# Four layers of linear and memory attention in one kernel: weight stores in pieces, one reciprocal later, the last block by quarters

## The chip, the cores and the metric

The kernel runs on one NeuronCore of a Trainium2 chip. The metric is the device time of one execution in microseconds (us), lower is better. The engines are named as in the profile: PE (TensorE, matrix products and transpositions), DVE (VectorE), ACT (ScalarE), POOL (GpSimd) and SP (SyncE, whose queue issues nearly all DMAs). PE, DVE, ACT and POOL each run their instructions in order.

## What is computed

`x` is 2048 tokens by 512 features in fp32. Four layers follow each other, A, B, A, B, with the same weights for both A and both B, and each adds its result to `x`:

```
x = x + A(layernorm(x));  x = x + B(layernorm(x));  x = x + A(layernorm(x));  x = x + B(layernorm(x))

A (32 heads of 16):  q, k, v = x @ wqkv;  pq, pk = q @ w_phi, k @ w_phi   (16 x 16 per head)
   phi = [softmax(p), softmax(-p)];  kv = phi_k^T v;  z = sum of phi_k
   o = (phi_q kv) / (phi_q z + 1e-6);  result o @ wo

B (32 heads of 16, 4 segments of 512 tokens):  q, k, v = x @ wq, x @ wk, x @ wv;  phi(t) = t + 1 or exp(t)
   in a segment:  a_dot = softmax(q k^T / 4, causal) v;   a_mem = (phi(q) M) / (phi(q) z + 1e-6)
   o = g a_mem + (1 - g) a_dot;   M += phi(k)^T v;  z += phi(k);   result o @ wo
```

## The kernel before

Products that must be exact to fp32 are done as three products of high and low parts (`mm3`, L465: high x high, high x low, low x high); the high part is a copy on ACT, the low part a subtraction on DVE or POOL. All work of the four layers is one stream for PE. Instructions of DVE, ACT, POOL and SP go through the helper `Ordered` (L161; every one of them bears the line L171 in the profile), and products through `mm` (L190, line L193) or `tp` (L195, line L197), which keep the order in which the program issues them. So the program's order is the engines' order, and it is written out by hand.

**Banks.** Of the eight PSUM banks, three bear the tag `g` (projections, transpositions, outputs), `lg` takes two (one tile of 128 x 1024 logits), and `mx`, `my` and `pv` one each.

**A layers.** `pass1` (L682) goes through the segments in the order 1, 2, 3, 0: values, keys, queries, features, and `kv` (L752) sums into `mx` and `my`. In the first A layer `first` (L618) splits the weights `awv`, `awk`, `awq` into high and low parts, and puts (store, tile) pairs of 1 MB into the list `owed` (L631); `settle` (L271) issues stores from it, one at every fourth step of the segment with n = 1 (L809). `prepare` (L320) meanwhile splits and stores the B layers' weights. In the second A layer these weights come back through `load_w` (L248), which goes through the whole of `bring` (L254) at once: eight loads of 256 KB. This second A layer starts under the end of the first B layer: `pass1` is then the generator `after`, from which the table `LAST` takes steps ("ln", "v", "n").

**B layers.** A segment s has four chunks c of eight heads and each chunk two halves: m = 0 to 31 counts (s, c, half). Five steps k belong to each m (R = 5, 160 in all). In every step `attend` (L1214) makes one block of logits into `lg`, ACT takes the exponential of 128 x 1024, and POOL masks the diagonal. Nine steps ahead `maxima` (L1172) makes the same logits per query in `mx` and `my` and takes maxima of them on DVE ("junk" and "mx" in the profile, result `mxs`), which `put_maxima` (L1205) turns and adds to the queries as a further row. `weighted` (L1250) multiplies the exponentials with the values into `pv`: key blocks 0 and 3 at step 5(m+1), blocks 1 and 2 two steps later (L1477); then ACT scales `pv` to `U`.

The denominators make a way through DRAM: `gather` (L1093) stores `U`'s rows, and `invert` (L1064) loads them compactly (`dm`, or `dn` when the memory's go along), inverts them on DVE (`flip`), stores the inverse (`put`), copies it wide (`spread`) and loads it wide (`load`). `INVERT` (L50) has the steps of these five, the first row for all segments but the last; half steps are those after the step's table entries (`due(k + 0.5)`, L1495). POOL then multiplies and joins (`close`, L1102, times in `JOIN`), and `out` (L1318) multiplies with the output weights.

In the last segment the chunks c >= 2 go another way: `finish` (L1283) turns `U` on PE, takes the reciprocal of the turned denominators on DVE and multiplies; `end_turn` (L1296) turns back, adds the memory's part, and splits into high and low; `early` (L1330) makes the last segment's output products over the first three chunks beforehand, and `end` (L1346) those over the last chunk, adds and stores. After the last step the end is: `finish` of m = 31, the rest of `early`, `end_turn(3)`, `end` (L1499 to 1511), with steps of the next layer between them.

**The tables** `FIRST`, `GAPS`, `LAST`, `FINAL` (L59 to 109) name for each step "m.j" the other work: "k2/3" is three of four parts of the key projection of chunk 2, "~" puts its subtraction behind, "max" is `put_maxima`, "n", "ln", "N" are steps of the normalisation, "t" and "a", "m" belong to the memory, "out", "p", "pt", "fin" to the outputs, "w" loads two pieces of the output weights, "v" in `LAST` is a step of `after`. `steps` (L1372) goes through them.

Of the kernel before, what the change touches and what calls it, by code (L numbers as in the profile page):

```python
# [17 lines left out]
DH = 16  # L18
# [41 lines left out]
0.1 max k2/2       | 0.2 v3/2          | 0.3 k2~  # L60
0.4 v3             | 1.0 m0            | 1.1 max q3/2      | 1.3 q3~           | 1.4 t1 k3/1
2.1 max k3         | 2.2 m1            | 2.3 ln~           | 2.4 ln~ ln~
3.3 q0+/2          | 3.0 w
3.1 max ln~        | 3.4 t2 q0+~ w
4.0 w | 5.2 w
4.1 max k0+/2 load | 4.2 m2            | 4.3 k0+/1         | 4.4 k0+
5.0 n              | 5.3 q1+/2 n
5.1 max v0+        | 5.4 t3 q1+~       | 6.2 m3 n
6.1 max v1+        | 6.3 k1+/2
6.4 a0+ k1+        | 7.0 n             | 7.2 n  # L70
7.1 max q2+~       | 7.3 v2+/2 n       | 7.4 t0+ v2+
"""
GAPS = """
0.1 max k2/3       | 0.2 n             | 0.3 k2~ v3/2 n
0.4 a1 v3          | 1.0 m0 n
1.1 max q3/3       | 1.2 n             | 1.3 q3~ k3/2      | 1.4 t1 k3~
2.1 max out/3      | 2.2 m1            | 2.3 ln ln         | 2.4 a2 ln x0
3.1 max ln out~    | 3.3 q0+/3 x1      | 3.4 t2 q0+~ k0+/2
4.1 max k0+~ out/1 load                | 4.2 m2            | 4.3 out~ x2
4.4 a3 q1+~  # L80
5.0 n              | 5.1 max out/3     | 5.3 out v0+/2 n x3
5.4 t3 v0+ k1+/1
6.1 max k1+~       | 6.2 m3 n          | 6.3 out/3
6.4 a0+ out v1+/2  | 7.0 n
7.1 max v1+ q2+/1 begin                | 7.2 n             | 7.3 q2+~ n N
7.4 t0+ v2+ N
# [3 lines left out]
0.1 max k2/3       | 0.2 n             | 0.3 k2~ v3/2 n  # L90
0.4 a1 v3 n        | 1.0 n             | 1.2 n
1.1 max q3/3 n     | 1.3 q3~ k3/2 n    | 1.4 k3~ n
2.1 max out/2      | 2.3 out/1         | 2.4 a2 x0
3.1 max ln~ ln~    | 3.3 out ln~ out/1 x1 | 3.4 out/1 ln~
4.1 max out~ v/2   | 4.3 out/3 x2      | 4.4 a3 out~ v x3
5.1 max out/3      | 5.3 fin out v/2   | 5.4 v pre
6.1 max v/2        | 6.3 fin v         | 6.4 v/2
7.1 pt p v         | 7.3 fin v/2 p     | 7.4 p v
"""
FINAL = """  # L100
0.1 max k2~        | 0.3 v3/3          | 0.4 a1 v3
1.1 max q3/2       | 1.3 q3~           | 1.4 k3/1
2.1 max k3/2       | 2.3 k3 out/1      | 2.4 a2 out/2 x0
3.1 max            | 3.3 out/2 x1      | 3.4 out/2
4.1 max out~       | 4.3 out/3 x2      | 4.4 a3 out/1
5.1 max out/2 x3   | 5.3 fin out~      | 5.4 pre
6.1 max            | 6.3 fin           | 6.4
7.1 pt p           | 7.3 fin p         | 7.4 p
"""
BEFORE = {-25: "q0 load", -23: "v0", -21: "k0",  # L110
          -18: "n", -17: "v1 n", -16: "n", -15: "n n", -14: "q1 n", -13: "n", -12: "k1 n", -11: "n", -10: "v2 n",
          -4: "max q2~", -1: "t0"}
# [3 lines left out]
def interleave_kernel(ctx, tc, x_in, a_wqkv, a_wphi, a_wo, b_wq, b_wk, b_wv, b_wo, b_beta,  # L116
# [496 lines left out]
    class LayerA:  # L613
# [4 lines left out]
        def first(self, hT, vv, upcoming):  # L618
# [63 lines left out]
        def pass1(self, first):  # L682
# [277 lines left out]
    class LayerB:  # L960
# [289 lines left out]
        def weighted(self, m, last):  # L1250
# [3 lines left out]
            if not last:  # L1254
                self.pv[m] = PS("pv", PV)
# [316 lines left out]
```

## Time and profile before

| | us |
|---|---|
| three runs | 1453.22, 1457.74, 1453.77; median 1453.77 |
| profiled execution | 1457.08, of it span 1455.4 |
| first A layer, to about | 260 |
| first B layer, about | 260 to 756 |
| second A layer, about | 756 to 1010 |
| second B layer, about | 1010 to 1455 |

All times in what follows count from the span's start. A row of the timeline has start, duration, engine, line, operation, output <- input by the program's names and the shape, and in square brackets the engine's idle time before it with what ended it. A row of the waits has the engine and what it wrote, what it waited for, and total, count and longest. A row of the windows has the stretch, its length, busy time (and instructions) of PE, PE's weight loads, DVE, ACT and POOL, then PE's granted clock as a share of full speed, the DMA engines' share and GB/s. "SPq" is a DMA issue on SP's queue. The profile calls weight tiles of the first A layer `w` or `e` by their buffers, the sum over keys `my<-P,v`.

### The profile page before, as it was taken

Reading aid. Unit: us, or ns where it says so; the run is one execution under the profiler, and the core shown is the slowest. Engines: PE = TensorE matmul, PEld = TensorE weight load, DVE = VectorE, ACT = ScalarE, POOL = GpSimd, SP = SyncE. Lnnn points to the kernel's source line nnn. Section 1 sums busy time; section 2 is a strip of 40 time slices with the busy share of each in tenths; the row PEclk is TensorE's granted clock in tenths of the full one; section 3 lists DMA queues with packets and bytes.
Section 4 is the critical chain, followed back from the end, with each engine's and each line's share of the span. In section 5 each row is a group of like instructions: output and inputs, shape, how many; then the busy total and the mean of one; then the engine's idle time right before and its main releaser. Section 6 shows DMA issues by size and latency. Waiting matters only on the chain.

```text
span 1455.4 us, 33122 instructions
## 1 busy us (share of the span) xinstructions
PE 1384.2 (95%) x12052; PEld 954.6 (66%) x12052; DVE 951.7 (65%) x3007; ACT 809.4 (56%) x1228; POOL 733.3 (50%) x1066
## 2 busy tenths in 40 slices
PE   7989999999999999998999998999999999999987
PEld 6878778765556565665568887886655566566544
DVE  4766788677467557566547767959756665666662
ACT  5546345447576576565544434553656865765653
POOL 1558765325456556444424456641445555654543
PEclk9999999999999999999999999999999999999999
DMA  5376475536546556566531103854465565556552
GB/s 191 117 290 233 138 234 171 177 115 191 165 139 211 170 150 201 153 181 201 184 136 55 59 30 112 274 185 134 120 197 149 150 213 172 156 173 185 143 167 72
DMA packets 139793, 236.34 MB, mean 162 GB/s; under 512 B 26576, under 2 KB 40016, under 8 KB 138864
## 3 DMA queue, kind: packets, MB, share of 16 engines
q1 hardware_dynamic: 138480, 233.70, 52.2%
q8 instruction: 97, 1.59, 0.4%
q10 hardware_dynamic: 1152, 0.52, 0.1%
q14 instruction: 64, 0.52, 0.1%
HBM read 129.17 MB, written 55.18 MB: 127 GB/s over the span
## 4 chain that ended last, share of the span: by engine, by line
PE 74%; DVE 7%; DMA 6%; ACT 6%; POOL 3%; issue 2%; SPq 1%; ACTq 0%; POOLq 0%; DVEq 0%
PE g L193 46%; PE pv L193 8%; PE lg L193 8%; PE mx L193 4%; PE g L197 4%; PE my L193 3%; ACT P L171 2%; PE lg L197 2%; SPq L171 1%; POOL P L171 1%; DVE junk L171 1%; DMA KN<-wide 1%; POOL tmp L171 1%; DMA dm<-den 1%; ACT tb L171 1%
## 5 line engine op out<-in xcount | busy, mean ns | idle before, releaser
L171 ACT ACTIVATE P<-lg 128x1024 f32<-128x1024 f32 x320 | 329.0, 1028 | 178.1 <-PE lg L193 164.3
L171 POOL TENSOR_SCALAR_AFFINE_SELECT P<-P 128x256 f32<-128x256 f32 (+1 forms) x448 | 191.2, 442 | 404.1 <-ACT P L171 403.3
L171 DVE CUSTOM_DVE_ANT_0 junk<-mx,mask 128x128 uint8<-128x128 f32 (+2 forms) x384 | 146.7, 420 | 124.2 <-PE my L193 93.4
L193 PE MATMUL g<-hh,wqk 128*128 128x512 f32 x512 | 186.3, 412 | 0.7 <-ACT mt L171 0.7
L193 PE MATMUL lg<-e,e 64*128 64x256 f32 (+2 forms) x1024 | 169.2, 388 | 14.4 <-ACT P L171 14.0
L193 PE MATMUL g<-w,oh 128*128 128x512 f32 x512 | 172.7, 419 | 4.4 <-ACT oh L171 4.0
L193 PE MATMUL pv<-P,v 128*32 128x512 f32 (+3 forms) x2048 | 167.2, 444 | 5.1 <-ACT ot L171 5.1
L171 DVE CUSTOM_DVE_ANT_0 mx<-mx,mask 128x512 f32<-128x512 f32 x128 | 89.1, 696 | 109.5 <-PE my L193 91.4
L193 PEld LDWEIGHTS lg<-e,e 64*128 64x128 f32 x1024 | 81.5, 185 | 114.4 <-issue 54.6
L193 PE MATMUL mx<-e,e 63*128 63x256 f32 (+2 forms) x512 | 145.5, 337 | 9.1 <-DVE mxs L171 8.5
L193 PE MATMUL my<-e,e 63*128 63x256 f32 (+2 forms) x512 | 147.3, 348 | 4.9 <-DVE mxs L171 3.7
L171 DVE CUSTOM_DVE_ANT_0 junk<-my,mask 128x128 uint8<-128x128 f32 (+2 forms) x384 | 146.8, 420 | 0.2 <-PE g L193 0.2
L193 PE MATMUL g<-w,hh 128*128 128x512 f32 x448 | 145.5, 406 | 0.0
L193 PEld LDWEIGHTS pv<-P,v 128*32 128x32 f32 x2048 | 55.0, 110 | 109.2 <-issue 95.8
L193 PEld LDWEIGHTS g<-hh,wqk 128*128 128x128 f32 x512 | 97.2, 190 | 31.8 <-issue 10.5
L193 PEld LDWEIGHTS g<-w,oh 128*128 128x128 f32 x512 | 90.0, 192 | 32.9 <-issue 11.0
L193 PE MATMUL g<-w,ol 128*128 128x512 f32 x256 | 103.8, 406 | 3.8 <-DVE ol L171 2.5
L193 PEld LDWEIGHTS mx<-e,e 63*128 63x128 f32 x512 | 90.0, 187 | 18.4 <-DVE mxs L171 7.3
L193 PE MATMUL g<-hl,wqk 128*128 128x512 f32 x256 | 101.1, 395 | 0.0
L171 DVE DVE_READ_ACCUMULATOR2_ANT mxs<- 128x1 f32 x1024 | 100.1, 98 | 0.0
L193 PEld LDWEIGHTS g<-w,hh 128*128 128x128 f32 x448 | 82.2, 192 | 22.6 <-issue 6.0
L193 PEld LDWEIGHTS my<-e,e 63*128 63x128 f32 x512 | 84.0, 187 | 17.9 <-DVE mxs L171 9.1
(167 smaller groups left out, 2820.9 us busy)
## 6 DMA issues: line engine op xcount, KB each, us to landing
e<-ta SPq DMA_DIRECT2D x384, 128.0 KB
wqk<-wqk SPq DMA_DIRECT2D x64, 512.0 KB
x<-x SPq DMA_DIRECT2D x48, 256.0 KB
wide<-inv SPq DMA_DIRECT2D x20, 512.0 KB
xr<-x SPq DMA_DIRECT2D x32, 256.0 KB
x<-xr SPq DMA_DIRECT2D x28, 256.0 KB
tmp<-U SPq DMA_DIRECT2D x56, 128.0 KB
KN<-wide SPq DMA_DIRECT2D x28, 256.0 KB
```

The costliest lines, as they stand in the source:

```text
L171: i = f(*a, **k)
L193: return held(nc.tensor.matmul(*a, **k))
L197: return held(nc.tensor.transpose(*a))
```

## The change

1. `owed` gets pieces of 256 KB (24 in place of 6 of 1 MB), and they are stored at every third step in the segments n = 1 and 2.
2. `INVERT` has three rows. For the first segment `flip` is at 4 and not 3.5: eight reciprocals of `dm`, four in each B layer, stand behind the four "junk" maxima that they stood ahead of. The steps of the other segments stay.
3. The second A layer's `awv` comes in pieces: from the 12th step of its normalisation on two loads of 256 KB a step, between SP's other DMAs.
4. `kv(0)` of an A layer's last segment is one projection earlier (`KV`).
5. Tables: the number of parts is written out everywhere; the first piece of the output weights comes at 2.2 and not at 3.0 of `FIRST`, one "n" of `GAPS` a few steps later, "max" ahead of or behind its neighbour in two cells.
6. `WEIGHTS`: of m = 30 the blocks 1, 2 come one step after 0, 3 (and not two); of m = 31 block 0 two steps, blocks 3 and 1 one step before the end of the steps, block 2 at it.
7. `final`, the second B layer alone: of the last eight blocks of logits every second goes to `mx` and `my`, with two exponentials of 128 x 512.
8. `close_last` takes the place of `finish(31)`, `end_turn(3)` and `end` in both B layers: `U`, the transpositions, reciprocals, sums and splits of the last chunk go in quarters of 128 tokens, in the order of `TAIL`.

DVE gets 24 instructions more, ACT 16, SP 18; PE and POOL have as many as before. The diff without the rewritten tables, where those change only as said in 5:

```diff
-INVERT = ((2.5, 3.5, 4.5, 5.5, 7.5), (2.5, 4.5, 5.5, 6.5, 8.5))
+INVERT = ((2.5, 4, 4.5, 5.5, 7.5), (2.5, 3.5, 4.5, 5.5, 7.5), (2.5, 4.5, 5.5, 6.5, 8.5))
+TAIL = "p o0 p o1 p o2 p t0 p o3 p t1 P a0 t2 a1 t3 a2 a3"
+WEIGHTS = {-2: ((0, (0, 3)), (1, (1, 2))), -1: ((-2, (0,)), (-1, (3, 1)), (0, (2,)))}
+SECOND = 9
+EARLY = (0, 1, 2)
+WV = 12
+SPREAD = 3
+KV = (4, 6)
...
-                owed.extend(zip(kept[key], w))
+                owed.extend((k[:, kc, :], t[:, kc, :]) for k, t in zip(kept[key], w) for kc in range(NC))
...
                 norm = norm_T(self.xsrc, SEGS[0], hTs, slow=True, off=True)
-                for _ in range(11):
-                    next(norm)
+                wv = []
+                weights = bring(wv, "awv")
+                for n, _ in enumerate(norm):
                     yield
-                wv = load_w("awv")
-                for _ in norm:
-                    yield
+                    if n + 1 >= WV:
+                        next(weights, None)
+                for _ in weights:
+                    pass
...
-                        if n == 1 and i % 4 == 0:
+                        if n in (1, 2) and i % SPREAD == 0:
                             settle(1)
...
-                    if t in (5, 6):
-                        add = kv(t - 5)
+                    if t in KV:
+                        add = kv(KV.index(t))
...
-                self.invert(s, c, k + READ[2], range(1, 2), INVERT[1])
+                self.invert(s, c, k + READ[2], range(1, 2), INVERT[2])
...
-            self.invert(s, c, k, range(2 if s > 0 else 1), INVERT[s == NSEG - 1])
+            self.invert(s, c, k, range(2 if s > 0 else 1), INVERT[0 if s == 0 else 2 if s == NSEG - 1 else 1])
...
-            for kbs, r in (((0,), 0), ((0,), 1), ((1, 3), 0), ((1, 3), 1), ((2,), None)):
-                pb = PS("lg", 1, (P, 2, 512))
+            for n, (kbs, r) in enumerate((((0,), 0), ((0,), 1), ((1, 3), 0), ((1, 3), 1), ((2,), None))):
+                left = R * 8 * NSEG - R * m - n
+                if self.final and left < SECOND and left % 2 == 0:
+                    pb = [PS(tag, 1) for tag in ("mx", "my")]
+                else:
+                    pb = PS("lg", 1, (P, 2, 512))
...
-                    act.activation(pr, pb, AF.Exp, scale=0.25)
+                    for part in enumerate(pb) if isinstance(pb, list) else ((slice(0, 2), pb),):
+                        act.activation(pr[:, part[0]], part[1], AF.Exp, scale=0.25)
...
-                U = T2("U", 2)
-                act.activation(U, self.pv.pop(m), AF.Identity, scale=share[:, m % 8 : m % 8 + 1])
+                U, pv = T2("U", 2), self.pv.pop(m)
+                for part in range(4 if m == 8 * NSEG - 1 else 1):
+                    cut = slice(part * P, part * P + P) if m == 8 * NSEG - 1 else slice(0, 512)
+                    act.activation(U[:, cut], pv[:, cut], AF.Identity, scale=share[:, m % 8 : m % 8 + 1])
...
+        def close_last(self, rest):
+            s, c, hf = NSEG - 1, NC - 1, 1
+            U, ot, old = self.U.pop(8 * NSEG - 1), self.ot.pop(c), self.old.pop((s, c))
+            hi, lo = self.oT[s, c] = self.outputs(s, c)
+            banks = [PS("mx", 1), PS("my", 1)]
+            wide = PS("lg", 1, (P, 2, 512))
+
+            def own(t):
+                cut = slice(t * P, t * P + P)
+                pt = banks[t % 2][:, t // 2 * P : t // 2 * P + P]
+                tp(pt, U[:, cut], ident)
+                r = T2("r", 4, shape=(P, 4, 4))[:, 0]
+                dve.reciprocal(r, pt.rearrange("p (h e) -> p h e", h=4)[:, :, 31 * hf])
+                dve.tensor_tensor(out=ot.rearrange("p q (h d) -> p q h d", d=DH)[:, t, 4 * hf : 4 * hf + 4], op=MUL,
+                                  in0=pt.rearrange("p (h d x) -> p h d x", h=4, x=2)[:, :, :, 1 - hf],
+                                  in1=r.unsqueeze(2).broadcast_to([P, 4, DH]))
+
+            def turned(t):
+                cut = slice(t * P, t * P + P)
+                pt = wide[:, t % 2, t // 2 * P : t // 2 * P + P]
+                tp(pt, ot[:, t], ident)
+                dve.tensor_tensor(out=old[:, cut], in0=pt, in1=old[:, cut], op=ADD)
+                act.copy(hi[:, cut], old[:, cut])
+                dve.tensor_tensor(out=lo[:, cut], in0=old[:, cut], in1=hi[:, cut].bitcast(F32), op=SUB)
+
+            def added(t):
+                po = PS("g", G)
+                for _ in self.product(po, s, t, range(NC - 1, NC)):
+                    pass
+                dve.tensor_tensor(out=self.xe[t], in0=po, in1=self.xe[t], op=ADD)
+                sync.dma_start(out=self.xdst[4 * s + t], in_=self.xe[t])
+
+            for what in TAIL.split():
+                if what == "p":
+                    next(rest, None)
+                elif what == "P":
+                    for _ in rest:
+                        pass
+                else:
+                    dict(o=own, t=turned, a=added)[what[0]](int(what[1]))
...
+            weights = {}
+            for m in range(N):
+                for j, kbs in WEIGHTS.get(m - N, ((0, (0, 3)), (2, (1, 2)))):
+                    weights.setdefault(R * (m + 1) + j, []).append((m, kbs))
...
-                if k % R in (0, 2) and 0 <= k // R - 1 < N:
-                    parts.insert(1, [lambda: self.weighted(k // R - 1, k % R == 2)])
+                if k in weights or k in memory["m"]:
+                    parts.insert(1, [lambda a=a: self.weighted(*a) for a in weights.get(k, ())])
...
-            self.finish(N - 1)
-            for _ in early:
-                pass
-            for _ in range(2):
-                next(after, None)
-            self.end_turn(NC - 1)
-            next(after, None)
-            self.end()
+            self.close_last(chain(early, (next(after, None) for _ in range(3))))
```

More of the change, by code (lines that the diff above doesn't have):

```diff
@@ L75 @@
[L75 to L85, printed above, removed]
@@ L115, in interleave_kernel @@
+2.1 max k3/2 | 2.3 k3/1 out/1 | 2.4 a2 out/2 x0
+3.1 max | 3.3 out/2 x1 | 3.4 out/2
+4.1 max out/1~ | 4.3 out/3 x2 | 4.4 a3 out/1
+5.1 max out/2 x3 | 5.3 fin out/2~ | 5.4 pre
+6.1 max | 6.3 fin
+7.1 pt p/3 | 7.3 p/3 fin | 7.4 p/3
+"""
+BEFORE = {-25: "q0 load", -23: "v0", -21: "k0", -18: "n", -17: "v1 n", -16: "n", -15: "n n", -14: "q1 n", -13: "n", -12: "k1 n", -11: "n", -10: "v2 n", -4: "max q2~", -1: "t0"}
 @with_exitstack
@@ L1248, in attend, with weighted @@
                 yield
-        def weighted(self, m, last):
+        def weighted(self, m, kbs):
             s, c, hf = m // 8, m % 8 // 2, m % 2
             v = self.vv[s][0]
-            if not last:
+            if kbs[0] == 0:
                 self.pv[m] = PS("pv", PV)
             pv, pr = self.pv[m], self.pr[m]
-            for kb in ((1, 2) if last else (0, 3)):
+            for kb in kbs:
                 for r in range(2):
@@ L1341, in early @@
                 po = PS("g", G)
-                yield from self.product(po, s, t, range(NC - 1))
+                yield from self.product(po, s, t, EARLY)
                 wait(lambda po=po, x=self.xe[t]: dve.tensor_tensor(out=x, in0=po, in1=x, op=ADD))
                 yield
-        def end(self):
-            s = NSEG - 1
-            for t in range(4):
-                po = PS("g", G)
-                for _ in self.product(po, s, t, range(NC - 1, NC)):
-                    pass
-                dve.tensor_tensor(out=self.xe[t], in0=po, in1=self.xe[t], op=ADD)
-                sync.dma_start(out=self.xdst[4 * s + t], in_=self.xe[t])
         def opening(self):
```

71 lines of the change are left out of this document (31 added, 40 removed).

## The prediction, made before the changed kernel had run

> **What bounds the kernel now.** I read the first part of the page, then the waits of the matrix engine (PE), then its timeline around each long wait, then the busy time by window with the granted clock.
>
> ```profile
> span 1455.4 us, 33122 instructions
> ...
> PE 1384.2 (95%) x12052; PEld 954.6 (66%) x12052; DVE 951.7 (65%) x3007; ACT 809.4 (56%) x1228; POOL 733.3 (50%) x1066
> ```
> PE is the bound, and the change leaves its work alone: the same products, some of them in another order. So time can come only from PE's idle 71.2 us (1455.4 - 1384.2) and from busy time that is slower than it need be. Of its waits two rows stand out, each as total, times and longest:
>
> ```profile
> PE mx L193 <- DVE mxs L171: 8.5, 5, 3.7
> PE my L193 <- issue: 6.2, 2, 4.2
> ```
> Both hold a few long waits. The timeline gives their places (start, duration, in brackets the idle time before):
>
> ```profile
> 84.83 0.33 PE L193 MATMUL my<-P,v 128*32 128x32 f32 x6 [4.21 <-issue]
> 370.10 0.76 PE L193 MATMUL mx<-e,e 63*128 63x512 f32 x1 [2.27 <-DVE mxs L171]
> 684.79 0.58 PE L193 MATMUL mx<-e,e 63*128 63x256 f32 x1 [3.71 <-DVE mxs L171]
> 1082.63 0.46 PE L193 MATMUL mx<-e,e 63*128 63x512 f32 x1 [1.97 <-DVE mxs L171]
> 729.64 0.74 PE L193 MATMUL g<-w,oh 128*128 128x512 f32 x2 [1.60 <-ACT oh L171]
> 1402.84 1.29 PE L193 MATMUL pv<-P,v 128*32 128x512 f32 x16 [1.48 <-ACT ot L171]
> ```
> And the windows behind them (the number after POOL's is PE's granted clock):
>
> ```profile
> 83.00:90.00 7.00, 5.17 (x20) 4.13 (x20) 1.11 (x2) 0.91 (x2) 3.57 (x7) 0.51 1.03 341
> 370.00:377.00 7.00, 6.90 (x31) 3.73 (x32) 3.56 (x16) 1.71 (x2) 0.91 (x3) 0.52 0.63 169
> 377.00:384.00 7.00, 7.00 (x53) 4.35 (x52) 4.13 (x16) 5.03 (x8) 2.66 (x4) 1.00 0.44 129
> 684.00:691.00 7.00, 6.14 (x17) 4.48 (x17) 3.40 (x14) 0.27 (x1) 0.00 (x0) 0.52 0.80 238
> 1083.00:1090.00 7.00, 6.78 (x32) 3.73 (x31) 3.12 (x14) 1.71 (x2) 0.77 (x2) 0.52 0.60 174
> 732.00:735.00 3.00, 3.00 (x8) 1.94 (x7) 1.65 (x4) 0.00 (x0) 0.00 (x0) 0.50 0.21 47
> 1403.00:1410.00 7.00, 6.32 (x55) 3.09 (x49) 5.12 (x17) 4.22 (x7) 3.79 (x6) 1.00 0.56 168
> 1425.00:1428.00 3.00, 3.00 (x20) 1.85 (x13) 0.23 (x1) 0.52 (x2) 3.00 (x4) 0.50 0.22 83
> 1449.00:1452.00 3.00, 2.64 (x7) 1.53 (x5) 1.71 (x3) 0.00 (x0) 0.00 (x0) 0.52 0.47 180
> ```
> Behind each of the four waits of 1.97 to 4.21 us the clock stands at half for a whole window of 7 us, and behind 1.60 for 3 us; behind 1.48 it stays full. So a long wait costs twice: its own time, and 7.00 x (1 - 0.52) = 3.4 us of work done slowly. The first three edits aim at exactly these four places.
>
> The sum is made against the profiled execution, 1457.08 us (span 1455.4 and 1.7 around it). The median of the runs is 3.3 below it, about one slow window; which windows the other runs had is not shown.
>
> **(a) Weight stores of the first layer in pieces.**
>
> ```profile
> 73.42 0.92 SPq L171 DMA_DIRECT2D awv<-w  x2
> 74.38 1.10 SPq L171 DMA_DIRECT2D awk<-w  x1
> 76.88 1.37 SPq L171 DMA_DIRECT2D awk<-w  x1
> ...
> 76.00:83.00 7.00, 4.61 (x142) 3.76 (x141) 4.40 (x8) 4.45 (x9) 6.88 (x8) 1.00 0.99 386
> ```
> Four stores of 1 MB are issued within 4 us; the transfers are then 0.99 busy at 386 GB/s, and PE stops for 4.21 us on "issue", which is nothing that the profile names, in the middle of 128 like matmuls of which 122 had run. The only thing that these lack is their own instructions, and both instruction queues move through the same transfer engines. I take the stop for a fetch behind 4 MB of stores. After: 24 stores of 256 KB, one every third step over two segments, so that at most one stands ahead of a fetch: 256 KB / 386 GB/s = 0.7 us. Gain 4.21 - 0.7 = 3.5, and the clock's 7.00 x 0.49 = 3.4: **6.9**. Bounds: 7.6 above; 0 if other traffic holds the fetch; -9 if the 18 DMAs that SP (the queue that issues nearly all) has more, at some 0.5 us each (0.92 for two in the row), all delayed what stands behind them. I take no delay, since three steps lie between two of them.
> [...]
>
> **(b) The first segment's reciprocals half a step later**, four in each B layer.
>
> ```profile
> 366.93 0.33 SPq L171 DMA_DIRECT2D dm<-den  x1
> 368.97 0.35 DVE L171 RECIPROCAL dm<-dm 128x32 f32<-128x32 f32 x1 [5.19 <-DMA dm<-den]
> ```
> VectorE (DVE) works in order: it stood 5.19 us at the reciprocal until the compact denominators had landed, with four maxima behind it whose products PE had long delivered; PE needs their banks. After, those four run first, and PE's next product starts 2.27 us (first layer) and 1.97 us (second) earlier. What is late next: the reciprocal still waits for its data at 368.97, and the following pair of maxima stands behind it.
>
> ```profile
> L171 DVE CUSTOM_DVE_ANT_0 junk<-mx,mask 128x128 uint8<-128x128 f32 (+2 forms) x384 | 146.7, 420 | 124.2 <-PE my L193 93.4
> ```
> Four maxima take 4 x 0.42 = 1.7 us and end ahead of 368.97. The next pair's products would then start at 370.10 - 2.27 = 367.8 and the first end by 368.6 (0.76); DVE is free for it at 368.97 + 0.35 = 369.3, 0.7 late, mostly under PE's next weighted sum (1.28, a row in (d)). I leave 0.5 a layer. The store of the inverse, which stands behind six other DMAs on SP, moves by less than the half step. Gain 2.27 + 1.97 - 1.0 = 3.2 and two windows of 3.36: **9.9**. Bounds: 0 (the next pair's wait is as long as the old one) to 10.9.
>
> **(c) The second A layer's value weights two pieces at a time.**
>
> ```profile
> 671.68 4.75 SPq L171 DMA_DIRECT2D w<-awv  x8
> 679.51 0.43 SPq L171 DMA_DIRECT2D dm<-den  x1
> 683.73 0.35 DVE L171 RECIPROCAL dm<-dm 128x32 f32<-128x32 f32 x1 [4.24 <-DMA dm<-den]
> ```
> Eight loads (2 MB) go out in 4.75 us ahead of the load of the denominators, which then needs 683.73 - 679.94 = 3.8 us to land; in (b) the same load took 1.7. DVE waits 4.24, PE 3.71. This reciprocal isn't moved; only the traffic before it is spread over the norm's steps, so the denominators' load and the stores around it stand ahead of most pieces on SP. Late next are the last pieces; their reader is the value product behind the norm, and one piece late costs it 0.7 (256 KB, as in (a)). At the same place of the second B layer, which has no such weights, PE has no wait of this kind. Gain 3.71 and 3.36: **7.1**; the bound from below is 0, if two of the pieces still stand just ahead.
>
> **(d) The end of the first B layer.** Half of the last-but-one weighted sum comes a step later, that of the last block earlier; the last output is made by quarters.
>
> ```profile
> 735.57 1.28 PE L193 MATMUL pv<-P,v 128*32 128x384 f32 x16
> 737.09 0.56 PE L193 MATMUL lg<-e,e 64*128 64x256 f32 x4 [0.23 <-ACT P L171]
> 755.15 0.73 PE L193 MATMUL g<-w,oh 128*128 128x512 f32 x2 [0.79 <-ACT oh L171]
> 1443.13 0.42 DVE L171 TENSOR_TENSOR tmp<-g,r 128x256 f32<-128x256 f32 x1
> 1451.68 0.69 DVE L171 TENSOR_TENSOR tb<-g,tb 128x512 f32<-128x512 f32 x1 [0.59 <-PE g L193]
> ```
> The weighted sum now covers the exponential between two logits that share one bank; gone from there, PE waits about 1.28 + 0.23 - 0.3 = 1.2. Moved into the 1.60 it fills 0.5. The 0.79 goes. In the quarters a chain is: an add of 0.69 queued first on DVE, add, ACT copy, subtraction of some 0.25 each (the rows with 256 and 512 columns, halved) and hand-overs, near 2.0, with one quarter's product of 0.95 as cover: waits of 0.2, 1.0 and 1.0. Net 0.5 + 0.8 - 1.2 - 2.2 = **-2.1**. Bounds: +2.8 (no wait is left and the slow window at 732 goes, 1.5) to -16.6 (the chain below wholly in series).
>
> **(e) The end of the second.** The same tail, and each second logits block uses the maxima's banks.
>
> ```profile
> 1414.36 0.51 PE L193 MATMUL lg<-e,e 64*128 64x512 f32 x2 [0.88 <-ACT P L171]
> 1418.36 0.56 PE L193 MATMUL lg<-e,e 64*128 64x256 f32 x4 [0.89 <-ACT P L171]
> 1423.60 0.50 PE L193 MATMUL lg<-e,e 64*128 64x512 f32 x2 [1.18 <-ACT P L171]
> 1422.63 1.27 POOL L171 TENSOR_TENSOR tmp<-tmp,KN 128x512 f32<-128x512 f32 x1 [1.67 <-DMA mmq<-wide]
> 1441.40 0.69 ACT L171 ACTIVATE U<-pv,share 128x512 f32<-128x512 f32 x1 [3.54 <-PE pv L193]
> 1446.94 0.73 PE L193 MATMUL g<-w,oh 128*128 128x512 f32 x2 [1.59 <-ACT oh L171]
> ```
> With two places for logits these three waits (2.95) can go. But the work that PE would do sooner needs the GpSimd product at 1422.63, which waits for a DMA that doesn't move; half of it, 1.5, is kept. From the last weighted sum to the last add took 1441.40 to 1452.37, 11.0; by quarters 10.5, with ACT, DVE and PE each at one quarter of their work. **+2.0**. Bounds: -3 to +5 (the slow windows at 1425 and 1449 go too, 1.5 each).
>
> The rest at nothing. The output weights' first step a few steps earlier puts two DMAs ahead of others on SP, hidden under PE's projections; uncovered, 2 x 0.6 (4.75 / 8 in (c)) = 1.2. One normalisation a step later on ACT is hidden by that step's exponential; uncovered, 0.7 by the ACT row at 1441.40. In the A layers the first sum of keys goes ahead of one projection on PE; its features are made a projection before, and uncovered it waits for at most that projection's 12 products, 12 x 0.37 (0.74 for two at 729.64) = 4.4.
>
> **Sum**: 6.9 + 9.9 + 7.1 - 2.1 + 2.0 = 23.8; 1457.08 - 23.8 = **1433.3 us**.
>
> **The rivals.**
> *The slow windows stay.* The waits go, but what lowers the clock is something else (the transfers that run there, or short waits that add up). For it: the window at 1425 follows waits of at most 1.18. Against: four of four long waits have it, and the rows at 377 and 1403 are full. Then 3.5 + 3.2 + 3.7 - 2.1 + 2.0 = 10.3, **1446.8**. [...]
> *The change doesn't do what it says*: the stop at 84.83 isn't the stores but the other traffic of that stage, and it stays with its window: 1433.3 + 6.9 = **1440.2**; or (c) stays, 1440.4.
> *Slower than before*: the quarters run in series. Place: the end of both B layers. One chain took 1441.40 to 1446.94, 5.5 us; if four small ones take as long each, because DVE, in order, stands at every ACT copy, that is 16.5 more a layer: 1433.3 + 33 = **1466**. It decides from 25 us, three quarters of that. Against: the sizes are a quarter, and other work is interleaved.
>
> **How the numbers follow.** Forecast, 1425 to 1440: 0.50. Windows stay: 0.20. A piece fails: 0.15. Quarters in series: 0.07. Gains and new waits cancel, 1450 to 1458: 0.08. Low end: 1433.3 less the left-overs (1.7), less (d)'s 2.1, less the three slow windows of the two ends (4.5) is 1425. High end: 1446.8 and 1 for it. About 0.3% is what a measurement of this kernel can tell from no change: faster 0.84, same 0.09, slower 0.07.
>
> **What would show it.** (a): no wait of PE on "issue" over 1 us near 80, and full clock there. (b): the reciprocal behind four maxima, PE's next product without wait. (c): the denominators land in 2 us. (d), (e): waits at the logits and before each of the last four sums. It is wrong if PE's clock is half at places without a wait, or if waits of 2 us turn up where none was.

## The result, and the profile after

The changed kernel took 1441.89 us (median; 1439.9 to 1443.21), the kernel before beside it 1453.49 (1453.04 to 1457.74): ratio 0.9913 with a 95% interval of 0.989 to 0.9935, 11.6 us less. In a later measurement it was 1446.16 against 1456.93, ratio 0.9934 (0.9907 to 0.9961). The forecast was 1433.3 in 1425 to 1448: faster, as said, with about half of the forecast gain.

The page of the kernel after, to be held against the one before. In the changed kernel the helper's line is L166, products bear L188 and transpositions L192.

```profile
span 1439.5 us, 33188 instructions
...
PE 1376.0 (96%) x12052; PEld 946.4 (66%) x12052; DVE 954.4 (66%) x3031; ACT 811.0 (56%) x1244; POOL 733.3 (51%) x1066
```
The profiled execution (1441.2 us) has a span 15.9 us shorter: PE's busy time fell by 8.2 at the same number of instructions, its idle time from 71.2 to 63.5, by 7.7.

The best view of where it came from is one row for each stretch between the same instructions of PE in both kernels. Columns: stretch, length, busy time (instructions) of PE, PE's weight loads, DVE, ACT, POOL, then the granted clock, the DMA share and GB/s. Before:

```profile
0.00:92.06 92.06, 77.61 (x631) 65.24 (x632) 51.44 (x103) 47.84 (x93) 40.30 (x65) 0.96 0.56 188
92.06:180.75 88.69, 88.40 (x1128) 72.37 (x1127) 65.14 (x99) 45.12 (x80) 67.49 (x72) 1.00 0.59 203
180.75:424.16 243.41, 233.00 (x1996) 164.64 (x1996) 174.20 (x563) 134.22 (x207) 112.21 (x165) 0.99 0.56 170
424.16:646.48 222.32, 216.43 (x1743) 134.28 (x1742) 142.53 (x571) 144.34 (x212) 125.86 (x198) 1.00 0.61 178
646.48:691.29 44.81, 39.66 (x271) 23.85 (x271) 27.71 (x113) 26.79 (x38) 19.20 (x37) 0.92 0.67 192
691.29:759.02 67.73, 63.60 (x404) 39.41 (x404) 30.50 (x96) 31.22 (x43) 23.48 (x36) 0.97 0.49 159
759.02:899.92 140.90, 137.32 (x1628) 112.44 (x1626) 100.77 (x162) 57.91 (x89) 69.33 (x74) 0.99 0.18 62
899.92:1137.06 237.14, 228.29 (x1939) 160.97 (x1940) 168.54 (x553) 130.79 (x201) 108.41 (x161) 0.99 0.57 172
1137.06:1406.18 269.12, 261.34 (x2070) 159.06 (x2068) 171.65 (x696) 173.33 (x248) 151.00 (x237) 1.00 0.59 173
1406.18:1455.40 49.22, 38.57 (x255) 22.29 (x254) 19.25 (x55) 17.87 (x22) 16.01 (x27) 0.93 0.28 92
```
After:

```profile
0.00:86.68 86.68, 75.69 (x630) 64.00 (x631) 51.84 (x103) 47.95 (x93) 39.79 (x65) 1.00 0.50 160
86.68:177.21 90.53, 88.46 (x1128) 72.23 (x1127) 65.13 (x99) 45.10 (x80) 67.87 (x73) 1.00 0.69 236
177.21:415.05 237.84, 230.17 (x1996) 163.28 (x1995) 174.17 (x564) 133.72 (x206) 111.71 (x165) 1.00 0.58 174
415.05:637.92 222.87, 216.70 (x1741) 134.32 (x1740) 142.06 (x569) 144.70 (x213) 126.27 (x198) 1.00 0.61 177
637.92:676.01 38.09, 36.71 (x272) 21.97 (x272) 28.00 (x114) 26.68 (x38) 19.22 (x37) 1.00 0.66 176
676.01:747.47 71.46, 64.90 (x405) 38.16 (x404) 31.59 (x108) 32.24 (x49) 23.38 (x36) 1.00 0.58 182
747.47:889.44 141.97, 137.16 (x1629) 112.21 (x1627) 101.01 (x164) 57.79 (x89) 69.30 (x74) 0.99 0.18 61
889.44:1121.12 231.68, 225.40 (x1939) 159.46 (x1940) 167.80 (x551) 130.32 (x200) 108.03 (x161) 1.00 0.60 176
1121.12:1391.02 269.90, 262.03 (x2069) 159.58 (x2069) 172.01 (x696) 173.22 (x249) 151.25 (x236) 0.99 0.60 173
1391.02:1439.50 48.48, 38.73 (x255) 21.19 (x254) 20.78 (x67) 19.28 (x33) 16.46 (x27) 0.96 0.27 93
```
Four stretches are shorter: 5.4 (the weight stores), 5.6 and 5.5 (the reciprocals, one in each B layer), 6.7 (the value weights); each has its clock back at 1.00. Five are longer: 1.8 behind the stores, 0.55, 3.7 (the end of the first B layer), 1.1 and 0.8. The last one is 0.7 shorter. 23.9 less 8.0 is the 15.9.

The long waits of PE that are left or new, from its timeline (idle time before, in brackets):

```profile
81.81 0.26 PE L188 MATMUL my<-P,v 128*32 128x32 f32 x6 [0.60 <-issue]
...
127.32 0.72 PE L188 MATMUL g<-e,hh 128*128 128x512 f32 x2 [1.54 <-ACT tb L166]
...
685.21 1.14 PE L188 MATMUL g<-w,hh 128*128 128x512 f32 x2 [0.93 <-DMA w<-awv]
...
723.20 0.56 PE L188 MATMUL lg<-e,e 64*128 64x256 f32 x4 [1.44 <-ACT P L166]
723.69 1.05 PE L188 MATMUL pv<-P,v 128*32 128x512 f32 x4
725.67 1.05 PE L188 MATMUL pv<-P,v 128*32 128x512 f32 x4 [0.93 <-POOL P L166]
...
879.66 0.33 PE L188 MATMUL my<-P,v 128*32 128x32 f32 x5 [2.65 <-issue]
...
1387.79 1.97 PE L188 MATMUL pv<-P,v 128*32 128x512 f32 x16 [2.05 <-ACT ot L166]
```
The 4.21 on issue is 0.60; the waits of 2.27 and 1.97 for the maxima are gone, and so is the 3.71. New are the 1.54 behind the stores, the 0.93 for the last value weights, and at the first end the 1.44 and 0.93; the 2.05 was 1.48. At 880 the stop on issue stands as before (2.03 there), with half clock behind it:

```profile
880.00:884.00 4.00, 4.00 (x14) 3.20 (x15) 1.66 (x4) 0.00 (x0) 2.37 (x3) 0.62 0.00 0
```

### The profile page after: what moved, and what is told of

Read it like the earlier page. It is cut to its first block, busy times and chain, and to the rows that moved or that the text cites. A ratio compares the mean times of both kernels' runs of the same rounds, so it can differ in the third digit from the quotient of the medians.

```text
span 1439.5 us, 33188 instructions
## 1 busy us (share of the span) xinstructions
PE 1376.0 (96%) x12052; PEld 946.4 (66%) x12052; DVE 954.4 (66%) x3031; ACT 811.0 (56%) x1244; POOL 733.3 (51%) x1066
## 3 DMA queue, kind: packets, MB, share of 16 engines
q8 instruction: 97, 1.59, 0.5%
## 4 chain that ended last, share of the span: by engine, by line
PE 71%; DMA 9%; DVE 8%; ACT 5%; POOL 3%; issue 2%; SPq 1%; ACTq 0%; POOLq 0%; DVEq 0%
PE g L188 44%; PE pv L188 8%; PE lg L188 7%; PE mx L188 4%; PE g L192 3%; PE my L188 3%; ACT P L166 2%; PE lg L192 2%; DMA wide<-inv 2%; POOL P L166 1%; SPq L166 1%; DVE junk L166 1%; DVE es L166 1%; DVE my L166 1%; DMA KN<-wide 1%
## 5 line engine op out<-in xcount | busy, mean ns | idle before, releaser
L166 ACT ACTIVATE P<-lg 128x1024 f32<-128x1024 f32 x316 | 324.9, 1028 | 177.6 <-PE lg L188 165.6
L166 POOL TENSOR_SCALAR_AFFINE_SELECT P<-P 128x256 f32<-128x256 f32 (+1 forms) x448 | 191.8, 444 | 386.7 <-ACT P L166 384.0
L166 DVE CUSTOM_DVE_ANT_0 junk<-mx,mask 128x128 uint8<-128x128 f32 (+2 forms) x384 | 147.0, 420 | 119.5 <-PE my L188 91.1
L188 PE MATMUL g<-hh,wqk 128*128 128x512 f32 x512 | 184.9, 410 | 0.7 <-ACT mt L166 0.7
L188 PE MATMUL lg<-e,e 64*128 64x512 f32 (+1 forms) x1010 | 166.4, 387 | 13.3 <-ACT P L166 11.9
L188 PE MATMUL pv<-P,v 128*32 128x512 f32 (+3 forms) x2048 | 168.1, 443 | 7.0 <-ACT ot L166 6.1
L188 PE MATMUL g<-w,oh 128*128 128x512 f32 x512 | 171.8, 417 | 1.8 <-ACT oh L166 1.3
L166 DVE CUSTOM_DVE_ANT_0 mx<-mx,mask 128x512 f32<-128x512 f32 x128 | 89.0, 695 | 108.4 <-PE my L188 94.0
L188 PE MATMUL my<-e,e 63*128 63x256 f32 (+3 forms) x519 | 148.6, 346 | 5.1 <-DVE mxs L166 4.0
L188 PEld LDWEIGHTS lg<-e,e 64*128 64x128 f32 x1010 | 80.0, 184 | 110.3 <-issue 51.8
L188 PE MATMUL mx<-e,e 63*128 63x256 f32 (+3 forms) x519 | 147.9, 337 | 2.1 <-DVE mxs L166 1.8
L166 DVE CUSTOM_DVE_ANT_0 junk<-my,mask 128x128 uint8<-128x128 f32 (+2 forms) x384 | 146.7, 419 | 0.3
L188 PE MATMUL g<-w,hh 128*128 128x512 f32 x448 | 144.0, 402 | 1.1 <-DMA w<-awv 0.9
L188 PEld LDWEIGHTS pv<-P,v 128*32 128x32 f32 x2048 | 54.6, 109 | 110.6 <-issue 92.4
L188 PEld LDWEIGHTS g<-hh,wqk 128*128 128x128 f32 x512 | 96.3, 188 | 31.4 <-issue 10.2
L188 PEld LDWEIGHTS g<-w,oh 128*128 128x128 f32 x512 | 88.1, 189 | 33.6 <-issue 12.9
L188 PE MATMUL g<-w,ol 128*128 128x512 f32 x256 | 102.3, 399 | 3.4 <-DVE ol L166 2.5
L188 PE MATMUL g<-hl,wqk 128*128 128x512 f32 x256 | 100.4, 392 | 0.0
L166 DVE DVE_READ_ACCUMULATOR2_ANT mxs<- 128x1 f32 x1024 | 99.8, 97 | 0.0
L188 PEld LDWEIGHTS mx<-e,e 63*128 63x128 f32 (+1 forms) x519 | 90.8, 186 | 11.7 <-DVE mxs L166 3.9
L188 PEld LDWEIGHTS g<-w,hh 128*128 128x128 f32 x448 | 80.6, 188 | 24.2 <-issue 6.3
L188 PEld LDWEIGHTS my<-e,e 63*128 63x128 f32 (+1 forms) x519 | 84.2, 186 | 18.4 <-DVE mxs L166 9.6
```

The source lines that it names most:

```text
L166: i = f(*a, **k)
L188: return held(nc.tensor.matmul(*a, **k))
```

## The experiments

Four questions: what each of the three edits is worth alone; what the ends bring; whether the stop on issue is a fetch; and whether the half clock is a cost outside of the one profiled execution too. Each kernel was timed on the same chip as the kernel before, whose time there stands beside its own.

**The kernel before, profiled once more.**

> The kernel before once more, for a second profile. If the long waits at 84.8, 370, 684.8, 890 and 1082.6 and the half-clock windows behind them belong to the program, they are here again within 0.3 us each, and the execution takes 1453 to 1458 us. If they are chance of one execution (the profiled one was 3.3 us above the median), some of them are missing, and the time is lower by about 3.4 us for each window that is missing.

1458.29 us. The waits are there again, at 3.34, 2.82, 4.10, 2.35 and 3.33, so they belong to the program, though their lengths move by up to 1.4 us and not the 0.3 expected. One window doesn't fit my term:

```profile
1085.02 0.46 PE L193 MATMUL mx<-e,e 63*128 63x512 f32 x1 [3.33 <-DVE mxs L171]
1086.00:1090.00 4.00, 4.00 (x26) 1.94 (x26) 1.16 (x5) 1.32 (x2) 0.00 (x0) 0.57 0.58 149
1085.00:1092.00 7.00, 6.75 (x41) 3.62 (x41) 3.43 (x16) 1.83 (x3) 0.77 (x2) 0.76 0.62 168
```
Behind a wait of 3.33, longer than the 1.97 of the first profile, half clock lasts about 3.4 us and not 6.8: 4.00 x (1 - 0.57) = 1.7 us are lost. So the loss was 3.4 behind the 1.97 and 1.7 behind the 3.33, and the length of the wait doesn't decide which. In the clock records of the two first profiles each stretch of half clock inside the span is 3.41 or 6.83 us long (four of each before, three of 3.41 after); losses in steps of 1.7, half of 3.41, agree.

**Each edit alone, on the kernel before.**

```diff
-INVERT = ((2.5, 3.5, 4.5, 5.5, 7.5), (2.5, 4.5, 5.5, 6.5, 8.5))
+INVERT = ((2.5, 4, 4.5, 5.5, 7.5), (2.5, 3.5, 4.5, 5.5, 7.5), (2.5, 4.5, 5.5, 6.5, 8.5))
...
```


> The kernel before with the three-row INVERT alone (eight reciprocals of the first segments behind the junk maxima). Theory, a long wait costs its own time and a window of half clock behind it: 2.27 + 1.97 less about 0.5 each and two windows of 3.36, near 10 us faster; the after trace showed 5.57 and 5.46 in the two stages, so 11. Rival, the clock would fall there anyhow: 3 to 4 us faster.

1451.34 against 1454.21, ratio 0.9972 (0.9952 to 0.9992): 2.9 us, at most 7. That is nearer to the rival's 3 to 4 than to the theory's 10 to 11, but not for the rival's reason: in the trace the wait of the first layer is gone and the clock stays full there. In the second layer a shorter wait is left, and 3.4 us of half clock begin 2 us behind it:

```profile
1079.39 0.38 PE L193 MATMUL mx<-e,e 63*128 63x256 f32 x1 [0.97 <-DVE mxs L171]
```

```diff
-                owed.extend(zip(kept[key], w))
+                owed.extend((k[:, kc, :], t[:, kc, :]) for k, t in zip(kept[key], w) for kc in range(NC))
...
-                        if n == 1 and i % 4 == 0:
+                        if n in (1, 2) and i % 3 == 0:
```


> The kernel before with the first layer's weight stores in pieces of 256 KB over two segments alone. Theory, the stop on issue at 84.8 is an instruction fetch behind 4 MB of stores: stop and window go, 5.4 us in the first stage, and the new 1.54 us wait on the copy of q at about 127 comes, so 3.5 to 4 us faster than before. My forecast had 6.9. Rival, the stop comes from other traffic: 0, or slower by 1.8.

1451.70 against 1454.21, ratio 0.998 (0.9958 to 1.0002): 2.5 us where the theory had 3.5 to 4, and not clear of none by itself. In its trace the stop at 84 is gone.

The third took the value weights' part of the diff as it stands above.

> The kernel before with the second A layer's value weights two pieces a step alone. Theory: wait and window at 684.8 go (6.7 us in the after trace), and the last pieces come late (0.93 at the value product), so 5 to 6 us faster. Rival, the wait there needs more than the weights moved: 0 to 3.

1452.07 against 1454.21, ratio 0.9979 (0.9961 to 0.9996): 2.1 us, within the rival's 0 to 3 and below the theory's 5 to 6, though in its trace the wait for the maxima at 684.8 is gone. That trace shows something else. Half clock begins at 1046.4, where PE had no wait longer than 0.27 us in the six us ahead (0.79 us idle in all):

```profile
1040.00:1046.00 6.00, 5.21 (x75) 3.16 (x74) 3.52 (x14) 4.79 (x8) 2.90 (x6) 1.00 0.38 123
1046.00:1050.00 4.00, 4.00 (x23) 2.28 (x25) 2.87 (x12) 2.90 (x4) 2.43 (x5) 0.57 0.48 103
```
The run below with the output weights two at a time has it at the same place (1044 to 1048, clock 0.57). So a long wait isn't the only thing that brings half clock; what brought it here stays open.

The three sum to 7.5 by medians and 10.5 by means, with an uncertainty of about 3 to 4 us each.

**The three together, without the rest of the change**, beside the changed kernel once more.

> The kernel before with the weight stores, the reciprocals and the value weights of the change, without the new ends, tables and the earlier sum of keys. If the three gains add up, the single runs give 3 to 4 us each, 10.5 in all: 1444. Then the new ends and tables are worth another 2 to 3. Rival, the new ends bring as much as the three together: 1448 or more.

> The changed kernel once more, as what the next ones are compared with, and for a second profile: 1440 to 1443 us. If what scatters the times is whether a long wait meets a slow window, this kernel, with three long waits where the kernel before has seven or more, must scatter less than the kernel before (a standard deviation of 3 us over 29 runs); if the scatter comes from elsewhere, as much.

The three alone: 1442.92 against 1456.93, ratio 0.9904 (0.9874 to 0.9933), 14.0 us. The whole change in the same measurement: 1446.16, 10.8 us, above the 1440 to 1443 expected. So the three edits are the gain, and the ends and tables bring nothing on top; by the medians they cost 3.2, though the two intervals overlap. The three together give no less than their sum, as the theory had it (10.5 expected); what it and the rival said of the ends, which were to bring a gain, falls. The scatter of the changed kernel there (1442.77 to 1454.55) was no smaller than that of the kernel before (1451.04 to 1463.05), so fewer long waits didn't steady it.

Each execution has its granted clock on record, and that says more than the medians. The clock lost in an execution, (1 - clock) x span, is on the mean 16.0 us in the fifteen of the kernel before, 8.8 in the nine of the changed kernel and 7.0 in the six with the three edits alone. Within a kernel the slower executions are those that lost more (correlation 0.89 in the kernel before, 0.87 in the changed one). So with the change half clock is rarer in the executions at large and not only in the profiled one, and the scatter goes with the half clock that an execution happens to meet. By itself this doesn't say which causes which, since a longer wait lengthens the time as well.

What the change's three edits leave behind shows in the traces. In the second profile of the whole change the maxima wait again, since the denominators' load, which waits for their store to land, came later in that execution (4.8 us behind the store's issue, 3.0 in the first profile):

```profile
368.18 0.38 PE L188 MATMUL mx<-e,e 63*128 63x256 f32 x1 [1.96 <-DVE mxs L166]
```
That is the rule and not the exception: in the five traces of the whole change without made waits (two with the output weights moved, one with the first end as it was) this wait in the first B layer is 0.26, 1.96, 2.06, 2.25 and 1.02, with half clock behind the last three, and in the three traces with the reciprocals moved but the old tables and ends it is 0.27, 0.27 and 0.26. So this may be part of what the whole change has more than its three edits; why the denominators land later with the new tables isn't shown.

In the kernel with the three alone the last pieces of the value weights come later than in the change:

```profile
685.88 1.13 PE L193 MATMUL g<-w,hh 128*128 128x512 f32 x2 [2.45 <-DMA w<-awv]
```

**The first end as it was**, in the changed kernel.

```diff
...
-                for j, kbs in WEIGHTS.get(m - N, ((0, (0, 3)), (2, (1, 2)))):
+                for j, kbs in (WEIGHTS if self.final else {}).get(m - N, ((0, (0, 3)), (2, (1, 2)))):
...
-            self.close_last(chain(early, (next(after, None) for _ in range(3))))
+            if self.final:
+                self.close_last(chain(early, (next(after, None) for _ in range(3))))
+            else:
+                self.finish(N - 1)
+                ...
+                self.end()
```


> The changed kernel with the first B layer's end as it was (weighted sums at the old steps, last output in whole tiles). Theory, the new end costs there: the traces have waits of 1.44 and 0.93 at the logits and the first weighted sum where 0.23 was, and 1.8 us more for the sums in parts, against 1.6 and 0.79 saved: 2 to 3 us faster than the changed kernel. Rival, the quarters pay: slower by 1 to 2.

1444.30 against the changed kernel's 1446.16 (ratios to before 0.9916, 0.9886 to 0.9947, and 0.9934): 1.9 us faster, just short of the theory's 2 to 3 and inside the noise. In the traces, from the layer's last turned maxima to the next layer's first turned tile, PE takes 40.8 us with the old end; with the new one 42.5, 41.6 and 42.5 in the three executions without a slow window there. That makes about 1.4, but on one execution of the old end: in the two traces of the kernel before with a single edit that have no slow window there either (the stores, the value weights), the old end takes 41.3 and 42.9. What is in every trace of the new end is a logits block that waits 1.44 or 1.45 for its bank. The 0.93 that the first weighted sum waits for the mask is in one of the four (0.17 in another).

**The stop on issue.** Two kernels move the loads of the output weights that stand ahead of the stop at 880.

```diff
-                        self.wo = load_w("awo")
+                        self.wo = []
+                        pieces = bring(self.wo, "awo")
...
+                        if 2 < t < 7 and n == 1:
+                            next(pieces)
```


> The changed kernel, with the second A layer's output weights (eight loads of 256 KB in one go, nothing else moves then) loaded two at a time over four projections. Theory, PE's stop on issue at 879.7 is a fetch of its instructions behind 2 MB of loads: the 2.65 us and the window of 1.7 behind go, 3 to 4.5 us faster than the changed kernel. Rival, the stop belongs to that place in the program: it stays, no change.

1446.69: no change. But it didn't test the theory, since the loads still went out together behind one wait of SP for PE (19.4 us), and the stop stayed:

```profile
875.02 4.03 SPq L166 DMA_DIRECT2D w<-awo  x8
...
885.41 0.26 PE L188 MATMUL my<-P,v 128*32 128x32 f32 x5 [2.10 <-issue]
```

```diff
-                        self.wo = load_w("awo")
...
                 if i < NT:
                     self.load_q(i + 4)
+                if i == 0:
+                    self.wo = load_w("awo")
```


> The changed kernel with the A layers' output weights loaded after the sums of keys and not before (a load of the second pass goes ahead of them on SP). In the run a_awo the eight loads still went out at once, since they wait for one buffer, so it didn't test this. Theory, PE's stop on issue near 880 is a fetch behind the 2 MB of loads: it goes, with its window, 3 to 4.5 us, and a wait for the late weights of 0 to 2 us may come in each A layer. Rival, the stop is of that place: it stays at 2 to 3 us.

Here the loads go out behind the sums, at 893, and the stop shrinks:

```profile
887.49 0.26 PE L188 MATMUL my<-P,v 128*32 128x32 f32 x5 [0.46 <-issue]
...
893.07 3.78 SPq L166 DMA_DIRECT2D w<-awo  x8
...
900.68 0.50 PE L188 MATMUL g<-w,oh 128*128 128x512 f32 x1 [1.93 <-DMA w<-awo]
```
The same instructions at the same place, with 123 of 128 ahead, wait 0.46 in place of 2.65 (1.1 to 3.5 in the eleven other traces without made waits). With the loads out of the way little of the stop is left, so most of it was the loads. What took its place is the wait for the weights themselves, 1.93 here and 1.27 in the first A layer, with half clock behind both, and the time is unchanged: 1446.71, ratio 0.9938 (0.9916 to 0.9959).

The page of the kernel before counts two instruction queues among those whose packets take the 16 DMA engines' time (packets, MB, share of 16 engines):

```profile
q8 instruction: 97, 1.59, 0.4%
q14 instruction: 64, 0.52, 0.1%
```
That PE waits for instructions is also in the traces' records of the transfers on q8, blocks of 16 KB (1.59 MB / 97). In all 22 stops on issue of more than 0.3 us within these bursts, in the twelve traces without made waits, PE goes on 1.24 to 1.60 us after such a block has landed: in the kernel before at 84.83 and 890.63, after blocks from 82.53 to 83.49 and from 888.31 to 889.31; here at 887.49, after one from 884.59 to 886.00. These blocks take 0.9 to 1.5 us each, and the one here is among the slowest. What differs is when they start: here 2.4 us ahead of the stop, at this place in the changed kernel 0.4 us after PE had stopped, and at the stores of the kernel before 1.9 us after. So, by these records, the stop is a fetch that starts late; that transfers ahead of it make it late is shown by moving them away (0.46 left). Behind 2 to 4 MB of weights these traces have the stop at 1.1 to 4.2 us.

**What a long wait costs in every execution.** Forty made waits in the changed kernel, short and long:

```diff
+                if k % R == 4 and 4 <= k // R < 24:
+                    pt, pz = PS("g", G), T2("pz", 1, shape=(P, P))
+                    tp(pt[:, 0:P], ident, ident)
+                    dve.tensor_copy(pz, pt[:, 0:P])
+                    for _ in range(2):               # 10 in the long one
+                        dve.tensor_copy(pz, pz)
+                    tp(pt[:, P : 2 * P], pz, ident)
```


> The changed kernel with 40 made waits, 20 in each B layer, one every fifth step: PE turns a tile, DVE copies it (128x128) three times in a chain, PE takes the result. Nothing else changes. The chain is some 1 us beside what DVE has queued, so waits of about 1 to 1.5 us, and few windows of half clock: the time grows by the waits, 40 to 60 us, and by no more than a few windows.

> The same with eleven copies in each chain, some 2 us longer. What a long wait costs in executions that aren't profiled is the difference to the short one. Theory, each of these waits has a window of half clock of 1.7 or 3.4 us behind it: 40 x 2 us of wait and 40 x 2.5 us of clock, 180 us slower than the short one. Rival, the clock is a matter of the profiled executions or of those places: 80 us slower.

The short ones took 1524.80 us, the long ones 1656.84: 132.0 more in timed executions. The waits (total, times, longest) and the page, of the short ones:

```profile
PE g L192 <- DVE pz L166: 57.2, 39, 3.2
...
span 1521.3 us, 33438 instructions
...
PE 1405.1 (92%) x12132; PEld 958.7 (63%) x12132; DVE 997.9 (66%) x3151; ACT 812.3 (53%) x1244; POOL 733.6 (48%) x1066
```
and the long ones:

```profile
PE g L192 <- DVE pz L166: 137.2, 38, 6.2
...
span 1656.4 us, 33755 instructions
...
PE 1456.8 (88%) x12132; PEld 979.7 (59%) x12132; DVE 1071.8 (65%) x3471; ACT 814.2 (49%) x1244; POOL 733.8 (44%) x1066
```
PE's idle time rose by 83.4 us (116.2 to 199.6), its busy time at the same instructions by 51.7, 135.1 together. The timed 132.0 are nearly the same sum, and the granted clock on record is 0.978 to 0.982 in the four executions of the short ones and 0.934 to 0.941 in the four of the long ones. So the half clock is paid in every one of these executions; one that nothing recorded isn't among them.

The short ones missed their forecast: 78.6 us above the changed kernel's 1446.16, not 40 to 60. Against its first profile they have 52.7 us more idle time, as expected, but 29.1 more busy time, with 80 products more. So waits of 57.2 / 39 = 1.5 us on the mean, the longest 3.2, bring some half clock too (granted clock 0.982 against 0.996). A long one (137.2 / 38 = 3.6) has 51.7 / 40 = 1.3 us more busy time than a short one. By the granted clock the two profiles differ by (1 - 0.937) x 1656.4 - (1 - 0.982) x 1521.3 = 77.0 us of lost clock, so one us of it cost PE about 0.67 us. The theory's 180 was too high, the rival's 80 too low: what is real is that half clock comes with the waits, and its mean price, 1.3 us more behind a long one than behind a short one, is well below 3.4.

**The value weights one step earlier**, on the kernel with the three edits.

```diff
-                    if n + 1 >= 12:
+                    if n + 1 >= 11:
```


> The kernel with the three edits alone, and the value weights' pieces from the 11th step of the normalisation on, one earlier. In b_three the last two pieces were issued so late that PE waited 2.45 us for them. Theory: that wait goes, and the denominators, now behind two more pieces, cost less than it: 1 to 3 us faster than b_three. Rival: the wait at the denominators comes back: no gain.

1442.81 against 1456.52, ratio 0.9909 (0.9880 to 0.9937). The wait of 2.45 is gone, and a little later another product waits 1.93 for ACT, with half clock behind:

```profile
688.12 1.28 PE L193 MATMUL pv<-P,v 128*32 128x512 f32 x16 [1.93 <-ACT ot L171]
```
No gain, as the rival had it, though the new wait isn't the one at the denominators that it named.

## Why the prediction was right, and where it was off

The direction, the three places and their order were right; the sum was 23.8 us against the profiled execution, where the traces have 15.9 and the timed medians 11.6. The measured 1441.89 lies above 1425 to 1440, to which I gave 0.50; it is inside the range only through the high end, and that I took from a rival whose mechanism isn't what happened. That part is luck.

- **(a)** 6.9 forecast. The stop is 0.60 in the first and 1.20 in the second profile (0.7 forecast) and its window is gone: 5.4 in that stretch. But 1.8 comes back behind it, where PE waits 1.54 for ACT's copy of the queries (0.34 to 1.54 in the eight traces with the pieces, none in the four without). 3.5 is left. That the stop is a fetch behind transfers was argued only in the forecast; the instruction queue's records show the fetch (PE went on at 84.83, 1.34 us after the block that landed at 83.49), and the loads at 880, taken away, show the transfers for the like stop there (0.46 left of it).
- **(b)** 9.9 forecast, 11.0 in the trace. The mechanism is right, but the 11.0 is the best of the draws: 0.3 and 0.6 are left over in the first profile (0.5 forecast), and in the first layer 1.0 to 2.25 in the four other traces of the new tables. The half step is just enough or too little, and how soon the denominators land moves by 2 us from one execution to the next.
- **(c)** 7.1 forecast, 6.7 in the stretch. What I named as late next, one piece at 0.7, is what came: 0.93, in other traces up to 2.45.
- **(d)** -2.1 forecast. The stretch is 3.7 longer, with (c)'s late pieces in it; the end alone costs about 1.4 by the experiment, which is not clear of the scatter. The wait at the shared bank (1.2 forecast) is 1.44. The quarters are better than forecast: waits of 0.16 and 0.49 at the first end in place of 0.2, 1.0 and 1.0, though at the second end one of 1.00 stands. What I missed is that the weighted sum, started ahead of its last mask, runs in two halves of four records that take 1.05 each, with 0.93 between them in this execution.
- **(e)** 2.0 forecast, 0.7 found, with one stretch of half clock fewer in it (1409 against 1425 and 1448); no run tests it by itself.
- **The rest at nothing** is 2.4 longer in the trace (0.55, 1.1 and 0.8); of these, 0.6 is a longer stop at 880 (2.65 against 2.03), which moves by more than that from trace to trace (1.1 to 3.5).

The step of mine that failed is the clock's term: 3.4 us for each wait, as if certain. It was 1.7 or 3.4, and the made waits of 3.6 us cost on the mean 1.3 more of it than those of 1.5. Even where the full 6.8 us of half clock went, it was worth less: the four windows were put at 13.5 us, and PE's busy time in their stretches fell by 1.9, 2.8, 2.9 and 2.9, 10.6 together. The profile before had a window of half the length too, behind the second of the two stops on issue, to which I gave no term:

```profile
890.63 0.26 PE L193 MATMUL my<-P,v 128*32 128x32 f32 x6 [2.03 <-issue]
892.00:896.00 4.00, 4.00 (x18) 3.42 (x17) 2.20 (x4) 0.67 (x2) 2.08 (x2) 0.57 0.18 49
```
Both profiles of the kernel before had high draws (lost clock 20.4 and 17.5 us, 14.8 on the mean of 29 executions), and I made the sum against one of them though I had seen its time 3.3 us above the median. In the trace after, three stretches of half clock are left: behind the stop of 2.65 at 880, behind the wait of 2.05 at 1388, and at 1409 behind 1.15 and 0.98. The rival "slow windows stay" gave 1446.8, nearer to the measured time than my forecast, and a piece that fails, 1440.2 or 1440.4, is nearer still. As mechanisms both fall: the stop at 84 and the wait at 684.8 are gone, the windows went with the waits in the trace, and in the probes they came with them. Of the first rival this much is left, that half clock can come without a long wait, as at 1046.

What stays open: whether the whole change is slower than its three edits at all. If it is, the traces name the wait for the maxima in the first B layer, up to 2.25 us and half clock behind it, beside the first end.

## What to carry to other kernels

Waits of the matrix engine of 2.27 and 1.97 us, with half clock behind them, had cost more than themselves here: without them the two stretches are 5.6 and 5.5 us shorter. When you sum such a wait, take a mean over profiles and not the window of the one at hand, and read the granted clock of every execution beside its time. A transfer that is taken out of one wait's way can end in front of another reader: here the weights that came too early for the denominators (3.71 us of wait, gone) came too late for their product (0.93 in the changed kernel, 2.45 with the three edits alone). And when an edit puts a product nearer to what makes its operands, ask how it runs when the second half of them is late (0.93 us between the two halves here).

## What the runs showed of the hardware

Half clock came behind waits of 1.97 us in the kernel before and of 0.97 us in the run with the reciprocals alone, while 1.48 and 1.54 had none. Most waits of some 2 us had it behind them (1.97, 2.03, 2.05 and 2.27 did, 1.96 in the second profile after and the 2.45 above did not), between 1 and 1.6 it went either way (1.60 had it), and at 1046 it came without any wait over 0.27.

A stop of PE on "issue" within a burst of 128 products of about 10 ns each ended 1.24 to 1.60 us after a 16 KB block of instructions had landed, in 22 of 22. At the first layer's stores that block started 0.9 to 1.9 us after PE had stopped in the four traces with stores of 1 MB, and 1.0 to 1.8 us before it stopped in the six traces with pieces that have a stop there at all.
